# Decode attention on one core: wq loaded first through the key and value places, all heads' queries computed at once, and a new order for the last head

## The chip, the cores and the metric

One core of one Trainium2 chip. The metric is device time in microseconds (us) of one execution; runs of one kernel agree within about 0.2%. A run's span is from its first to its last instruction.

TensorE is PE, its weight loads PEld, VectorE DVE, ScalarE ACT, GpSimd POOL; SP only issues transfers.

## The reference, cut to what matters

One token goes through a pre-norm attention block with a cache, then a pre-norm ReLU block.

```python
B, Sq, D = 1, 1, 640
H, Sk, Dh = 32, 32768, 192            # k_cache, v_cache: [1, 32, 32768, 192] bf16, 403 MB each
x = A_x
q = (layernorm(x) @ wq).reshape(B, Sq, H, Dh).transpose(0, 2, 1, 3)      # wq [640, 6144]
scores = einsum("bhqd,bhkd->bhqk", q, k_cache) * Dh ** -0.5
o = einsum("bhqk,bhkd->bhqd", softmax(scores), v_cache)
h = x + o.transpose(0, 2, 1, 3).reshape(B, Sq, H * Dh) @ wo              # wo [6144, 640]
return h + relu(layernorm(h) @ w1) @ w2                                  # w1 [640, 1536], w2 [1536, 640]
```

## The kernel before

Each head's keys come in two loads of 6.29 MB (places `kt[0]`, `kt[1]`, 48 KB a partition), its values in four of 3.15 MB (`vt[0]`, `vt[1]` in turn). PE transposes part of the keys and computes their scores; DVE computes the other scores by multiply and sum. Eight chunks of scores a head go through ACT's exponential, then PE sums values weighted by them ("PV" below). One program per engine; `g.wait(label)` waits for the labelled step. wq is loaded in four parts of eight heads each, in rows of 3 KB, and each head's query row is computed during the head before it (QG = 8).

The transfers (all on SP's queue):

```python
# ... (cut: load(), rows())
        def keys(h, ld):
            if h > 0:
                g.wait("PV", h - 1, 4 * ld + 1)
                g.wait("scs", h - 1, 4 * ld + 3)
            load(kt[ld][:], rows(k_hd, h, P * JK * ld, JK), f"dk{ld}", "k", h, ld)

        def vals(h, ld):

            if ld == 1 and h > 0:
                g.wait("PV", h, 0)
            elif ld > 1:
                g.wait("PV", h, 2 * ld - 3)
            elif h > 0:
                g.wait("PV", h - 1, 5)
            if h < LAST:
                src = rows(v_hd, h, P * JK * (ld // 2), JK)[:, (ld % 2) * JL * Dh:(ld % 2 + 1) * JL * Dh]
            else:
                src = rows(v_hd, h, P * JL * ld, JL)
            load(vt[ld % NV][:], src, f"dv{ld % NV}", "v", h, ld)

        load(wq_v, wq_view[:, :, 0:QG * Dh], "dwq", "wq", 0)
        for h in range(LAST):
            keys(h, 0)
            if h > 0:
                vals(h - 1, NL - 1)
            vals(h, 0)
            if h % QG == QG - 1:
                gq = (h + 1) // QG
                g.wait("PV", h - 1, 3)
                load(wq_v, wq_view[:, :, gq * QG * Dh:(gq + 1) * QG * Dh], "dwq", "wq", gq)
            keys(h, 1)
            vals(h, 1)
            vals(h, 2)
            if h % 2 == 0:
# ... (cut) the last head, whose keys and values come in smaller pieces:
        for ld in range(NL - 1):
            if ld != 1:
                g.wait("PV", LAST - 1, 2 * ld + 1)
                g.wait("scs", LAST - 1, 2 * ld + 3)
            end_keys(ld, P * JL * ld, JL, ("dk0", "dke0", "dk1")[ld])
            if ld == 0:
                vals(LAST - 1, NL - 1)
            else:
                vals(LAST, ld - 1)
        k0 = P * JL * (NL - 1)
        at = []
        for i, jl in enumerate(ENDJ):
            at.append((k0, jl))
            end_keys(NL - 1 + i, k0, jl, f"dke{1 + i}")
            k0 += P * jl
        vals(LAST, NL - 2)
        i = 0
        for ld, (k0, jl) in enumerate(at):
            for c, (l, off, jc, *_) in enumerate(ends):
                if l == NL - 1 + ld:
                    g.wait("PV", LAST, 1)
                    load(v_tile(LAST, l)[:, off * Dh:(off + jc) * Dh],
                         rows(v_hd, LAST, k0, jl)[:, off * Dh:(off + jc) * Dh], f"dve{i}", "vc", LAST, c)
                    i += 1
        g.wait("PV", LAST, 3)
        load(w1_s, B_w1.rearrange("(c p) n -> p c n", p=P), "dw1", "w1")
        g.wait("PV", LAST - 1, 4)
        for i, (c0, c1) in enumerate(zip(W2_CUTS[:-1], W2_CUTS[1:])):
            load(w2_s[:, c0:c1], B_w2.rearrange("(c p) n -> p c n", p=P)[:, c0:c1], f"dw2_{i}", "w2", i)
        g.wait("y_row")
```

The query of a head, as a row, spread over all partitions and as columns:

```python
    def q_rows(g, h, turn=None):

        g.wait("at", "wq", h)
        hh = h % QG if turn is None else turn % QG
        pe_group(g, [mmul(mm[0:1, 0:Dh], ln_t["ln1"]["xn"][:, c:c + 1], wq_v[:, c, bass.ds(hh * Dh, Dh)],
                          start=(c == 0), stop=(c == DT - 1)) for c in range(DT)], ("q", h), "pe_act")

    def q_spread(g, h):
        g.wait("row", h)
        calls = [mmul(mm[:, 0:Dh], ones_row[:], row_e[0:1, Dh:2 * Dh], start=True, stop=True)]

        i = Dh
        for b in range(3):
            for e in range(2):
                for off in (Dh + b * (2 * P - Dh), b * (2 * P - Dh)):
                    calls.append(mmul(mm[:, i:i + 1], row_e[0:1, off + e:off + 2 * P:2], ones_row[0:1, 0:1],
                                      start=True, stop=True))
                    i += 1
        pe_group(g, calls, ("qs", h), "pe_act")
```

PE's program for the last head:

```python
    def pe_end(g):
        h = LAST
        transposes(g, h, 0)
        den_mm(g, h - 1)
        scores_pe(g, h, 0)
        for c in range(1, NC - 2):
            transposes(g, h, c)
            values(g, *((h - 1, NC - 3 + c) if c < 3 else (h, c - 3)))
            scores_pe(g, h, c)
            if c == 3:
                o_turn(g, h - 1)
        transposes(g, h, 6)
        values(g, h, 3)
        for c in (7, 8, 9):
            transposes(g, h, c)
            if c > 7:
                values(g, h, c - 4)
            scores_pe(g, h, c - 1)
        values(g, h, 6)
        scores_pe(g, h, 9)
        values(g, h, 7)
        den_mm(g, h)
        values(g, h, 8)
        values(g, h, 9)
        o_turn(g, h)
        project(g, h + 1)
        # ... (cut: the projection, the second norm, h1, y)
```

The softmax here doesn't subtract the row's maximum and nothing guards it: scores larger than these inputs give would overflow.

Of the kernel before, what the change touches and what calls it, by code (L numbers as in the profile page):

```python
# [7 lines left out]
A = mybir.AluOpType  # L8
# [72 lines left out]
def kernel(  # L81
# [20 lines left out]
    eps = 1e-5  # L102
# [8 lines left out]
    QG = 8  # L111
# [3 lines left out]
    NV = 2  # L115
    LAST = H - 1
    assert Sk % (P * JK) == 0 and NK == 2 and NL == 4 and 2 * Dh == 3 * P and H % QG == 0 and H % 2 == 0 and H >= 4

# [25 lines left out]
    wq_view = A_wq.rearrange("(c p) n -> p c n", p=P)  # L144
# [14 lines left out]
    wq_s = sbuf("wq_s", [P, DT * QG * Dh], bf16, 512)  # L159
# [6 lines left out]
    pA = [sbuf(f"pA{i}", [P, J], bf16) for i in range(4)]  # L166
    pB = [sbuf(f"pB{i}", [P, J], bf16) for i in range(4)]
    x_row = sbuf("x_row", [DT, P], bf16)
    ident_b = sbuf("ident_b", [P, P], bf16)
    ident_f = sbuf("ident_f", [P, P], f32)  # L170
    ones_row = sbuf("ones_row", [1, P], bf16)
# [4 lines left out]
    row_e = sbuf("row_e", [1, 3 * Dh], bf16)  # L176
# [22 lines left out]
    wq_v = wq_s[:].rearrange("p (c n) -> p c n", c=DT)  # L199
# [5 lines left out]
    w2_s = wq_s[:, 0:FT * D].rearrange("p (f n) -> p f n", n=D)  # L205
    assert DT * Dff <= JL * Dh and FT * D <= DT * QG * Dh
# [10 lines left out]
    names += [f"dk{i}" for i in range(NK)] + [f"dv{i}" for i in range(NV)] + ["dwq", "dwo", "dx", "dout"]  # L217
    names += [f"dke{i}" for i in range(4)] + [f"dve{i}" for i in range(4)] + ["dw1"] + [f"dw2_{i}" for i in range(3)]
# [6 lines left out]
    def dma_program(g):  # L225
# [6 lines left out]
        def keys(h, ld):  # L232
            if h > 0:
                g.wait("PV", h - 1, 4 * ld + 1)
                g.wait("scs", h - 1, 4 * ld + 3)
            load(kt[ld][:], rows(k_hd, h, P * JK * ld, JK), f"dk{ld}", "k", h, ld)

        def vals(h, ld):

            if ld == 1 and h > 0:  # L240
                g.wait("PV", h, 0)
            elif ld > 1:
                g.wait("PV", h, 2 * ld - 3)
# [5 lines that stand above are left out]
                src = rows(v_hd, h, P * JL * ld, JL)  # L249
            load(vt[ld % NV][:], src, f"dv{ld % NV}", "v", h, ld)  # L250

        load(wq_v, wq_view[:, :, 0:QG * Dh], "dwq", "wq", 0)
        for h in range(LAST):
            keys(h, 0)
            if h > 0:
                vals(h - 1, NL - 1)
            vals(h, 0)
            if h % QG == QG - 1:
                gq = (h + 1) // QG
                g.wait("PV", h - 1, 3)  # L260
                load(wq_v, wq_view[:, :, gq * QG * Dh:(gq + 1) * QG * Dh], "dwq", "wq", gq)
            keys(h, 1)
            vals(h, 1)
            vals(h, 2)
            if h % 2 == 0:
                if h > 0:
                    g.wait("prj", h)
                load(wo_s[:], wo_view[h // 2], "dwo", "wo", h // 2)
# [20 lines left out]
        vals(LAST, NL - 2)  # L289
# [10 lines left out]
        g.wait("PV", LAST - 1, 4)  # L300
# [8 lines left out]
    def pool_program(g):  # L309
        e = nc.gpsimd  # L310
        g.do(lambda: e.memset(ident_b[:], 0.0), "pool_act", ("ident0",))
        g.wait("ident0")
        g.do(lambda: e.affine_select(out=ident_b[:], in_=ident_b[:], compare_op=A.not_equal, fill=1.0, base=0,
                                     pattern=[[-1, P]], channel_multiplier=1), "pool_row", ("ident",))
        g.wait("x")
        g.do(lambda: e.sem_inc(sems["pool_pe"], 1) if not g.planning else None)
        book_relay(g, "x")
        relay(g, "wq", 0)
        def key(h, ld):
            relay(g, "k", h, ld)  # L320
            g.do(lambda: nc.gpsimd.sem_inc(sems["pool_dve"], 1))  # L321
            book_relay(g, "k", h, ld, sem="pool_dve")

        for h in range(LAST):
            key(h, 0)
            if h > 0:
                relay(g, "v", h - 1, NL - 1)
            relay(g, "v", h, 0)
            relay(g, "wq", h + 1)
            key(h, 1)  # L330
            relay(g, "v", h, 1)
            relay(g, "v", h, 2)
            relay(g, "W", h)
        for ld in range(NL - 1):
            key(LAST, ld)
            if ld == 0:
                relay(g, "v", LAST - 1, NL - 1)
            else:
                relay(g, "v", LAST, ld - 1)
        relay(g, "v", LAST, NL - 2)  # L340

    def relay(g, *label):
        if label[0] == "wq":
            if label[1] % QG == 0:
                g.wait("wq", label[1] // QG)
        elif label[0] != "W":
            g.wait(*label)
        elif label[1] % 2 == 0:
            g.wait("wo", label[1] // 2)
        g.do(lambda: nc.gpsimd.sem_inc(sems["pool_pe"], 1))  # L350
        book_relay(g, *label)
# [69 lines left out]
    def values(g, h, c):  # L421
# [3 lines left out]
        if h == LAST and ld >= NL - 1:  # L425
            g.wait("vc", h, c)
        elif off == 0:
            g.wait("at", "v", h, ld)
        g.wait("ep", h, c)
# [5 lines left out]
        a, b = pA[c % 4], pB[c % 4]  # L435
# [37 lines left out]
    def q_rows(g, h, turn=None):  # L473

        g.wait("at", "wq", h)
        hh = h % QG if turn is None else turn % QG
        pe_group(g, [mmul(mm[0:1, 0:Dh], ln_t["ln1"]["xn"][:, c:c + 1], wq_v[:, c, bass.ds(hh * Dh, Dh)],
                          start=(c == 0), stop=(c == DT - 1)) for c in range(DT)], ("q", h), "pe_act")

    def q_spread(g, h):  # L480
        g.wait("row", h)
        calls = [mmul(mm[:, 0:Dh], ones_row[:], row_e[0:1, Dh:2 * Dh], start=True, stop=True)]

        i = Dh
        for b in range(3):
            for e in range(2):
                for off in (Dh + b * (2 * P - Dh), b * (2 * P - Dh)):
                    calls.append(mmul(mm[:, i:i + 1], row_e[0:1, off + e:off + 2 * P:2], ones_row[0:1, 0:1],
                                      start=True, stop=True))
                    i += 1  # L490
        pe_group(g, calls, ("qs", h), "pe_act")
# [4 lines left out]
    def pe_head(g, h, turn=None):  # L496
        for c in range(NC):
# [13 lines left out]
            if c == 5:  # L511
                q_rows(g, h + 1, turn)
            if c == 6:
                q_spread(g, h + 1)
# [5 lines left out]
    def pe_start(g):  # L520
        g.wait("at", "x")
        g.wait("identf")
        pe_group(g, [lambda: pe.transpose(out=mm[:, 0:4].bitcast(bf16)[:, 0:DT], in_=x_row[:],
                                          identity=ident_b[0:DT, 0:DT])], ("xT",), "pe_dve")
        pe_norm(g)
        pe_group(g, [mmul(attT[:, 0:DT], ident_b[:], zero5[:], start=True, stop=False, skip_group_check=True)],
                 ("att0",))
        g.wait("xn", "ln1")
        g.wait("at", "wq", 0)
        q_rows(g, 0)  # L530
        q_spread(g, 0)

    def pe_end(g):
        h = LAST
        transposes(g, h, 0)
        den_mm(g, h - 1)
        scores_pe(g, h, 0)
        for c in range(1, NC - 2):
            transposes(g, h, c)
            values(g, *((h - 1, NC - 3 + c) if c < 3 else (h, c - 3)))  # L540
            scores_pe(g, h, c)
            if c == 3:
                o_turn(g, h - 1)
        transposes(g, h, 6)
        values(g, h, 3)
        for c in (7, 8, 9):
            transposes(g, h, c)
            if c > 7:
                values(g, h, c - 4)
            scores_pe(g, h, c - 1)  # L550
        values(g, h, 6)
        scores_pe(g, h, 9)
        values(g, h, 7)
# [36 lines left out]
    def exp_pe(g, h, c):  # L590
        jp = chunks(h)[c][3]
        g.wait("S", h, c)
        g.do(lambda: act.activation(out=pB[c % 4][:, 0:jp], in_=sp[:, 0:jp], func=F.Exp, scale=SCALE,  # L593
                                    accum_out=dsums[:, 2 * c + 1:2 * c + 2]), "act_pe", ("ep", h, c))

    def exp_dve(g, h, c):
# [5 lines left out]
        g.do(lambda: act.activation(out=pA[c % 4][:, 0:jd], in_=sc[c % NC][:, 0:jd], func=F.Exp, scale=SCALE,  # L602
                                    accum_out=dsums[:, 2 * c:2 * c + 1]), "act_pe", ("ed", h, c))

    def q_row(g, h):
        g.wait("q", h)
        g.do(lambda: act.copy(out=row_e[0:1, Dh:2 * Dh], in_=mm[0:1, 0:Dh]), "act_pe", ("row", h))  # L607
# [14 lines left out]
    def act_start(g):  # L622
        g.do(lambda: act.dma_start(out=x_row[:], in_=A_x.rearrange("b s (c p) -> (b s c) p", p=P)), "dx", ("x",), by=16)
        act_norm(g, "ln1")
        q_row(g, 0)

    def act_head(g, h):
        q_wide(g, h)
        for c in range(NC if h < LAST else NC - 2):
# [3 lines left out]
            if c == 5 and h < LAST:  # L633
                q_row(g, h + 1)
# [81 lines left out]
    def dve_start(g):  # L716
        for t, v in ((ones_row, 1.0), (mean_mat, 1.0 / D), (eps_t, eps), (row_e, 0.0), (ones_mat, 1.0), (dsums, 0.0),
# [3 lines left out]
        g.do(lambda: dve.tensor_copy(out=ident_f[:], in_=ident_b[:]), "dve_pe", ("identf",))  # L721
        g.wait("xT")
        g.chain(lambda: dve.tensor_copy(out=x_col[:], in_=mm[:, 0:4].bitcast(bf16)[:, 0:DT]), "dve_row")
        dve_norm(g, "ln1", x_col)
# [154 lines left out]
```

## Time and profile before

| | before |
|---|---|
| time, median (range) of 3 runs | 1923.72 us (1923.21 to 1923.9) |
| span of the profiled execution | 1923.6 us (its time: 1925.44) |
| busy: PE, DVE, ACT | 81%, 81%, 50% |
| the queue of SP: share of the 16 DMA engines' span | 99.6% |
| bytes read | 824.97 MB, 429 GB/s over the span |

The prediction below shows the lines on the middle and the end. Of the start, this is the timeline of PE and SP (start us, length us, engine, line, operation, out<-in, form, count, and in brackets the idle time before and what ended it):

```profile
8.69 0.96 PE L368 MATMUL mm<-wq_s,xn_ln 128*1 128x192 bf16 x5 [3.67 <-POOLq L350]
...
23.07 3.46 PE L387 MATMUL tp<-ident_f,kt 128*128 128x128 f32 x15 [12.39 <-POOLq L350]
...
27.82 0.90 PE L368 MATMUL sp<-qm,kT 128*128 128x2 bf16 x30 [1.29 <-ACT kT L587]
```

The first query comes out of the first part of wq at 8.7 us; PE then waits 12.4 us for head 0's keys ("POOLq" in a bracket is GpSimd's sequencer, which passes on to the others that a load has landed). The 30 score matmuls, each with a weight load of its own ("128*128": 128 rows by 128 columns), take 0.90 us, 30 ns each.

### The profile page before, as it was taken

The numbers are of one execution on the slowest core, as the hardware profiler recorded it, in microseconds if no ns is written. First come the engines' busy times: TensorE is split into PE (matmuls) and PEld (weight loads), VectorE is DVE, ScalarE is ACT, GpSimd is POOL, SyncE is SP. The second block draws the span as 40 slices with busy tenths as digits, with TensorE's granted clock in tenths as the row PEclk, the third lists the DMA queues.
The fourth block names the chain that finished last, engine by engine and source line by source line (L and its number), as shares of the span: only waits on it lengthen the run. The fifth ranks groups of instructions, "written<-read, shape, count | busy, mean of one in ns | idle before, by whom it ended". The sixth has DMA issues, their size and how long they took to land.

```text
span 1923.6 us, 36300 instructions
## 1 busy us (share of the span) xinstructions
PE 1554.4 (81%) x15899; PEld 1088.3 (57%) x15899; DVE 1560.5 (81%) x734; ACT 966.9 (50%) x2031; POOL 0.7 (0%) x6
## 2 busy tenths in 40 slices
PE   4878878777888788787777878878878788787897
PEld 3555555555555565555555655655656556555564
DVE  5878888878888798787787878978879788888885
ACT  3544545544555454454454545544545445544553
POOL 0000000000000000000000000000000000000000
PEclk8989898887888887888888888888788798898888
DMA  9999999999999999999999999999999999999997
GB/s 408 433 428 434 435 430 440 429 430 435 429 435 437 426 436 432 432 437 429 438 430 429 438 429 433 439 428 433 431 433 435 430 433 436 431 437 432 430 410 328
DMA packets 35864, 825.25 MB, mean 429 GB/s; under 512 B 3588, under 2 KB 5124, under 8 KB 11140
## 3 DMA queue, kind: packets, MB, share of 16 engines
q1 hardware_dynamic: 35834, 824.98, 99.6%
q8 instruction: 12, 0.20, 0.0%
q14 instruction: 8, 0.07, 0.0%
q10 hardware_dynamic: 10, 0.00, 0.0%
HBM read 824.97 MB, written 0.00 MB: 429 GB/s over the span
## 4 chain that ended last, share of the span: by engine, by line
DMA 55%; PE 35%; ACT 6%; DVE 3%; SPq 1%; issue 0%; POOLq 0%; DVEq 0%
DMA kt<-in_A_k_cache_dram 54%; PE o_ps L368 19%; PE tp L387 10%; ACT kT L587 6%; PE sp L368 4%; PE mm L368 2%; DVE pr L672 1%; DVE sc L675 1%; DMA vt<-in_A_v_cache_dram 1%; PE attT L368 1%; SPq L227 1%; ACT pA L602 0%; POOLq L350 0%; DVE o_pair L686 0%; ACT row_e L607 0%
## 5 line engine op out<-in xcount | busy, mean ns | idle before, releaser
L672 DVE TENSOR_TENSOR pr<-kt,qb 128x2304 f32<-128x2304 bf16 (+2 forms) x257 | 755.9, 2941 | 303.9 <-POOLq L321 278.7
L587 ACT COPY kT<-tp 128x1024 bf16<-128x1024 bf16 (+1 forms) x899 | 817.3, 989 | 321.3 <-PE tp L387 320.4
L387 PE MATMUL tp<-ident_f,kt 128*128 128x128 f32 x3459 | 578.1, 334 | 240.8 <-POOLq L350 238.6
L675 DVE TENSOR_REDUCE sc<-pr 128x12 f32<-128x2304 f32 (+2 forms) x257 | 755.3, 2939 | 8.9
L387 PEld LDWEIGHTS tp<-ident_f,kt 128*128 128x128 f32 x3459 | 501.8, 174 | 252.4 <-POOLq L350 244.0
L368 PE MATMUL o_ps<-vt,pB 128*2 128x384 bf16 x2286 | 459.2, 351 | 7.9 <-POOLq L350 7.1
L593 ACT ACTIVATE pB<-sp 128x20 bf16<-128x20 f32 (+2 forms) x258 | 47.8, 185 | 571.5 <-PE sp L368 571.5
L368 PE MATMUL o_ps<-vt,pA 128*2 128x384 bf16 x1778 | 330.6, 326 | 0.0
L368 PEld LDWEIGHTS o_ps<-vt,pB 128*2 128x2 bf16 x2286 | 187.6, 88 | 233.5 <-issue 92.2
L368 PE MATMUL sp<-qm,kT 128*128 128x2 bf16 x6918 | 214.5, 164 | 106.6 <-ACT kT L587 106.3
L368 PEld LDWEIGHTS sp<-qm,kT 128*128 128x128 bf16 x6918 | 192.5, 98 | 187.6 <-ACT kT L587 144.8
L368 PEld LDWEIGHTS o_ps<-vt,pA 128*2 128x2 bf16 x1778 | 150.0, 84 | 142.0 <-issue 3.5
L602 ACT ACTIVATE pA<-sc 128x12 bf16<-128x12 f32 (+2 forms) x257 | 53.4, 208 | 41.4 <-DVEq L65 40.5
L593 ACT ACTIVATION_READ_ACCUMULATOR pB<-sp 128x1 f32 x258 | 50.2, 194 | 0.0
L602 ACT ACTIVATION_READ_ACCUMULATOR pA<-sc 128x1 f32 x257 | 48.7, 190 | 0.0
L686 DVE TENSOR_SCALAR o_pair<-o_ps,rec 2x384 bf16<-2x384 f32 x32 | 19.4, 605 | 6.3 <-PE o_ps L368 1.7
L368 PE MATMUL mm<-wq_s,xn_ln 128*1 (+1 forms) x160 | 18.7, 248 | 3.7 <-POOLq L350 3.7
L680 DVE TENSOR_REDUCE rec<-mm 128x1 f32<-128x20 f32 x32 | 5.7, 179 | 16.3 <-PE mm L368 11.8
L368 PE MATMUL attT<-oT,wo_s 128*128 128x1 bf16 x465 | 16.4, 164 | 0.3 <-DVE oT L696 0.3
L368 PEld LDWEIGHTS mm<-dsums,ones_mat 128*128 128x128 f32 x64 | 15.1, 291 | 0.3 <-issue 0.3
L368 PEld LDWEIGHTS attT<-oT,wo_s 128*128 128x128 bf16 x465 | 14.5, 101 | 0.4 <-DVE oT L696 0.4
L368 PE MATMUL mm<-ones_row,row_e 1*128 1x1 bf16 x384 | 14.0, 159 | 0.0
(71 smaller groups left out, 145.4 us busy)
## 6 DMA issues: line engine op xcount, KB each, us to landing
vt<-in_A_v_cache_dram SPq DMA_DIRECT2D x127, 3072.0 KB, 18.8
kt<-in_A_k_cache_dram SPq DMA_DIRECT2D x62, 6144.0 KB, 32.4
kt<-in_A_k_cache_dram SPq DMA_DIRECT2D x3, 3072.0 KB, 18.3
wq_s<-in_A_wq_dram SPq DMA_DIRECT2D x4, 1920.0 KB, 22.5
wo_s<-in_A_wo_dram SPq DMA_DIRECT2D x16, 480.0 KB, 9.5
kt<-in_A_k_cache_dram SPq DMA_DIRECT2D x1, 1920.0 KB, 15.4
kt<-in_A_v_cache_dram SPq DMA_DIRECT2D x2, 960.0 KB, 22.4
kt<-in_B_w_dram SPq DMA_DIRECT2D x1, 1920.0 KB, 16.7
```

Source lines behind the costliest of these rows:

```text
L227: g.do(lambda: nc.sync.dma_start(out=dst, in_=src), sem, label, by=16)
L368: return lambda: pe.matmul(o, lhsT=w, rhs=r, **kw)
L387: calls.append(lambda b=b, o=o: pe.transpose(out=dst[:, b, :], in_=src[:, o:o + 2 * P].bitcast(f32), identity=ident_f[:]))
L587: g.do(lambda: act.copy(out=kT[c % 2][:, b0:b0 + nb, :], in_=src[:, 0:nb, :].bitcast(bf16)), "act_pe", ("cp", h, c, k))
L593: g.do(lambda: act.activation(out=pB[c % 4][:, 0:jp], in_=sp[:, 0:jp], func=F.Exp, scale=SCALE, accum_out=dsums[:, 2 * c + 1:2 * c + 2]), ...
L602: g.do(lambda: act.activation(out=pA[c % 4][:, 0:jd], in_=sc[c % NC][:, 0:jd], func=F.Exp, scale=SCALE, accum_out=dsums[:, 2 * c:2 * c + 1 ...
L672: g.chain(lambda: dve.tensor_tensor(out=pr[:, 0:j1 - j0, :], in0=src[:, (off + j0) * Dh:(off + j1) * Dh].rearrange("p (j d) -> p j d", d=D ...
L675: g.chain(lambda: dve.reduce_sum(out=sc[c % NC][:, j0:j1], in_=pr[:, 0:j1 - j0, :], axis=X), "dve")
L680: g.chain(lambda: dve.reduce_sum(out=rec[:, 0:1], in_=mm[:, 0:2 * NCM], axis=X), "dve")
L686: g.do(lambda: dve.tensor_scalar_mul(out=o_pair[:, :, 1, :], in0=o_ps[0:2, 0:2 * Dh].rearrange("q (i d) -> q i d", i=2), scalar1=rec[0:2, ...
```

## The change

Its intent: load all of wq at the start in long rows, using places that are still free, so that no small rows come later and no query work lies in the heads; let the last head's second value load go as soon as its place is free; halve the third, and reorder the last head so that PE does not wait for it. The core of the diff:

```diff
-    wq_view = A_wq.rearrange("(c p) n -> p c n", p=P)
+    wq_view = A_wq.rearrange("(p c) n -> p (c n)", p=P)
-    pA = [sbuf(f"pA{i}", [P, J], bf16) for i in range(4)]          # pB likewise
+    pA = [sbuf(f"pA{i}", [P, J], bf16) for i in range(NB)]         # NB = 5
+    x_pc = sbuf("x_pc", [P, DT], bf16)
+    qe = sbuf("qe", [HE, 2 * H], bf16)                             # HE = Dh // 2 = 96
+    wq_c = [kt[1][:, c * H * Dh:(c + 1) * H * Dh] for c in range(DT - 1)] + [vt[1][:, 0:H * Dh]]
-    w2_s = wq_s[:, 0:FT * D].rearrange("p (f n) -> p f n", n=D)
+    w2_s = sbuf("w2_s", [P, FT, D], bf16, 512)
@@ transfers
         def keys(h, ld):
+            elif ld == 1:
+                g.wait("att0")
         def vals(h, ld):
-            if ld == 1 and h > 0:
+            if ld == 1 and h == LAST:
+                g.wait("vfree")
+            elif ld == 1 and h > 0:
                 g.wait("PV", h, 0)
-        load(wq_v, wq_view[:, :, 0:QG * Dh], "dwq", "wq", 0)
+        n = (DT - 1) * H * Dh
+        load(kt[1][:], wq_view[:, 0:n], "dwq0", "wq", 0)
+        load(vt[1][:, 0:H * Dh], wq_view[:, n:n + H * Dh], "dwq1", "wq", 1)
-            if h % QG == QG - 1:
-                gq = (h + 1) // QG
-                g.wait("PV", h - 1, 3)
-                load(wq_v, wq_view[:, :, gq * QG * Dh:(gq + 1) * QG * Dh], "dwq", "wq", gq)
-        vals(LAST, NL - 2)
+        g.wait("PV", LAST, 1)
+        src = rows(v_hd, LAST, P * JL * (NL - 2), JL)
+        n = J * Dh
+        load(vt[0][:, 0:n], src[:, 0:n], "dv0", "v", LAST, NL - 2)
+        load(vt[0][:, n:2 * n], src[:, n:2 * n], "dvh", "vh")
@@ PE
+    def queries(g):
+        for c in range(DT):
+            if c == 0 or c == DT - 1:
+                g.wait("wq", min(c, 1))
+            calls = [mmul(o_ps[0:HE, 2 * h + e:2 * h + e + 1], wq_c[c][:, h * Dh + e:(h + 1) * Dh:2],
+                          ln_t["ln1"]["xn"][:, c:c + 1], ...)
+                     for h in range(H) for e in range(2)]
@@ pe_start: ... queries(g), then att0; q_rows and its ACT copy are gone, q_spread reads qe
@@ pe_end
+        transposes(g, h, 1)
         scores_pe(g, h, 0)
+        values(g, h - 1, NC - 2)
+        values(g, h - 1, NC - 1)
+        pe_group(g, [mmul(attT[0:1, 500:501], ident_b[0:1, 0:1], zero5[0:1, 0:1], start=False, stop=True,
+                          skip_group_check=True)], ("vfree",))
+        scores_pe(g, h, 1)
+        ... (cut) transposes and scores run ahead, so that before values(4) only scores 8 and 9 are open:
+        transposes(g, h, 9)
+        values(g, h, 4)
+        scores_pe(g, h, 8)
+        scores_pe(g, h, 9)
+        for c in (5, 6, 7):
+            values(g, h, c)
@@ ACT
         g.do(lambda: act.dma_start(out=x_row[:], in_=A_x.rearrange("b s (c p) -> (b s c) p", p=P)), "dx", ("x",), by=16)
+        g.do(lambda: act.dma_start(out=x_pc[:], in_=A_x.rearrange("b s (p c) -> (b s p) c", p=P)), "dx2", ("x_pc",), by=16)
```

## The prediction

> **What bounds the kernel now.** I read the page first, for the busy shares. The transfers are the full resource: TensorE (PE) and VectorE (DVE) are busy 81% of the span, the one DMA queue 99.6%.
>
> ```profile
> q1 hardware_dynamic: 35834, 824.98, 99.6%
> HBM read 824.97 MB, written 0.00 MB: 429 GB/s over the span
> ```
>
> The key and value caches are 2 x 32 heads x 32768 x 192 x 2 bytes = 805.3 MB of these 825; wq and wo are 7.9 MB each, w1 and w2 2.0 MB each. A busy queue can still be one that waits for buffers, so next I read the chain of work that ended last, in order of time (start, length, what). The loads of the second half of a head's keys recur in it; start plus length is when one landed.
>
> ```profile
> 306.64 33.81 DMA kt<-in_A_k_cache_dram
> ...
> 365.21 33.38 DMA kt<-in_A_k_cache_dram
> ...
> 423.82 38.73 DMA kt<-in_A_k_cache_dram
> ...
> 489.70 30.90 DMA kt<-in_A_k_cache_dram
> ...
> 547.73 32.12 DMA kt<-in_A_k_cache_dram
> ```
>
> They landed at 340.45, 398.59, 462.55, 520.60 and 579.85, so 58.14, 63.96, 58.05 and 59.25 us apart. A head moves 25.17 MB, and every other head 0.49 MB of wo too: 25.17 MB in 58.1 us is 433 GB/s, and 25.66 MB in 59.25 us is 433 GB/s again. The same two intervals recur to the last head. A loop held by waits would not price half a megabyte of wo at exactly its bytes; so the middle is bound by bytes, and no work of an engine there is worth anything. The third load came after one of the four wq loads (1.97 MB in rows of 3 KB): 63.96 - 59.25 = 4.7 us, or 417 GB/s. At 433 it would have been 4.54 us. **The small rows of wq cost about 0.17 us a load, 0.7 us in all.**
>
> What remains outside the middle is the start and the end. Windows of the end (last two columns: DMA share, GB/s):
>
> ```profile
> 1868.00:1878.00 10.00, 9.29 (x80) 5.37 (x78) 9.56 (x7) 5.90 (x11) 0.00 (x0) 0.88 0.86 336
> 1902.00:1913.00 11.00, 10.83 (x100) 5.81 (x98) 0.48 (x3) 3.96 (x13) 0.00 (x0) 1.00 1.03 399
> 1913.00:1924.00 11.00, 5.18 (x146) 4.47 (x146) 2.24 (x13) 0.56 (x2) 0.00 (x0) 0.74 0.04 14
> ```
>
> In the first, (433 - 336) x 10 us = 0.97 MB is missing: 2.2 us without transfers. Windows of 1 us place it at 1870 to 1874 (221 and 25 GB/s at its bottom). The issues on the queue say why:
>
> ```profile
> 1848.12 0.43 SPq L227 DMA_DIRECT2D kt<-in_A_k_cache_dram  x1
> 1872.17 0.33 SPq L227 DMA_DIRECT2D vt<-in_A_v_cache_dram  x1
> 1872.54 1.72 SPq L227 DMA_DIRECT2D kt<-in_A_k_cache_dram  x3
> 1878.36 0.33 SPq L227 DMA_DIRECT2D vt<-in_A_v_cache_dram  x1
> ```
>
> For 24 us nothing is issued: the last head's second value load waits for that head's first values matmuls, although the matmuls that free its buffer are the previous head's last. Transfers then run without a gap to about 1913.3. The chain's last part:
>
> ```profile
> 1878.36 19.60 DMA vt<-in_A_v_cache_dram
> ...
> 1898.05 4.26 PE o_ps L368 x16
> ...
> 1912.86 0.62 DVE o_pair L686
> ...
> 1915.59 1.67 PE o_ps L368 x60
> ...
> 1917.61 1.73 PE attT L368 x60
> ```
>
> The third value load of the last head lands at 1897.95; PE idles 2.5 us before it, then has 14.8 us of work until its last values matmul (1912.84), then 10.8 us of short steps to the end. The last piece of w2 lands at about 1915.0 (issued 1904.7, 10.3 us to landing), 2.6 us before the matmuls on w2 begin. So the end is PE's, with the transfers close behind.
>
> **What the Trainium skill says.**
> - DMA: Bandwidth & Descriptors, section Where 436 GB/s comes from: sixteen ports give 435.2 GB/s. The trace's 433 agrees; the section's remark that HBM binds near 358 does not hold in this trace, with one core running.
> - Same page, section Why small descriptors are slow: a fixed overhead per packet. Agrees in kind: 3-KB rows at 417 against 433 GB/s; it is small at this size.
> - TensorE: Matmul & The Clock Gate, section What's actually happening: an idle window of about 3.4 us halves the clock. The trace has a granted clock of 0.50 from 1898 to 1901, just after the 2.5-us idle, and the 16 values matmuls took 4.26 us there against 2.7 at full clock; the exact threshold no view shows.
>
> **The change, part by part.**
>
> *All of wq first* (6.29 MB in 48-KB rows into the key place, 1.57 MB in 12-KB rows into a value place). No byte is saved: 5.90 MB, or 13.6 us at 433, move from the middle to the start, and head 0's keys land at about 36.4 instead of 22.97. Every later load moves early by what left the middle. Gain: the 0.7 us above. Added: x once more as 128 rows of 10 bytes, 8 per DMA engine, which I guess at 0.1 to 0.5 us. Net about -0.4.
>
> *The queries at once*: 320 matmuls with 96-column weights and one moving column. The like matmuls of the scores (sp, 30 in 0.90 us in the timeline) run at 30 ns each, so 9.6 us. The first 256 can start at about 18 (2.2 to the first byte, 14.5 for the bytes, 1.3 to landing); the last 64 wait for the second load at about 22, behind the first 256 which end near 25.7; done near 28. The second key load waits for this, but the queue still holds head 0's first keys and values until about 42. So nothing stalls.
>
> *Per head*, PE loses the five matmuls on wq and most of the 13 of the spreading (0.57 + 0.25 + 0.44 us in the timeline of head 0), ScalarE (ACT) a copy of 0.3 us. All beside transfers: 0 us on the end.
>
> *vfree*: the one-element matmul after the previous head's last values, near 1859 in the old timeline (after the scores at 1853.7, two values groups of 2.7 us). The load then goes out 13 us earlier, with two loads still ahead of it: the hole is closed, -2.2 us for all later transfers.
>
> *Halved third value load, new order, five probability buffers*: the old order waits at 1898.05 for the whole load. With the shift of -2.6 (0.4 + 2.2) the whole lands at 1895.3, its first half (1.57 MB, 3.6 us) at 1891.7. PE no longer waits for it: the last head's fourth key piece lands at about 1885.2 (1888.0 before), then, by old durations, transposes 2.1, values(3) 3.1, transposes 1.2; the copies of ACT (2.2 us) hold the scores to about 1893.8; scores 0.6, transposes 0.9: values(4) start near 1895.3. Left from there: 16 + 16 + 10 + 10 + 8 + 4 values matmuls at 163 ns = 10.4 us, scores(8) and (9) 0.8, the wait for the exponential between them 0.4, the sum 0.3: 12 us, so the last values end near 1907.4 instead of 1912.84. The last value pieces land by about 1903, in time. DVE's last scores move from 1899.0 to about 1897.5: in time. The 10.8 us of short steps stay: 1918.2. w1 lands near 1907.4, needed near 1910.2; w2 ends near 1912.4, its matmuls would end near 1913.9. The end is still PE's, with 1.5 us in hand.
>
> *w2 in a buffer of its own*: removes a wait already fulfilled; 0.
>
> **Sum**: the profiled span goes from 1923.6 to 1918.2, -5.4 us: about 2.6 from the transfers, 2.8 from the shorter PE tail after them. The times lie 0.1 above the span: 1918.3.
>
> **Rivals.**
> 1. *The transfers become the end's bound.* w2 with 1280-byte rows lands last. For: the 399 GB/s of the second window, and only 1.5 us in hand. It sets a floor: 1912.4 + 0.4 for the last matmuls + 4.3 to the end = 1917.1. No faster PE tail gets below it unless the transfers themselves gain more.
> 2. *The clock.* If PE idles before values(4) and drops to half clock as at 1898, 1.6 us or more of the gain is lost: 1920. For: the old trace does this often. Against: the new order fills the idle.
> 3. *Head 0.* Between 22.97 and the landing of head 1's first keys (76.2) 22.5 MB moved, 52.0 us at 433: 1.2 us were lost, I think since head 0's third value load (issued at 48.8) came just too late behind work at half clock. The whole stretch now comes 13.4 us later with the same order, and another phase of the clock: from -1.2 to +1.5.
> 4. *Queries stall the second key load*: only if a query matmul takes over 75 ns ((42 - 18) us / 320). At 160 ns it would add some 27 us (1945), still within 2%. The scores' 30 ns speak against it.
> 5. *Everything hidden*: only wq's rows count, and the tail is eaten by DVE or ACT: 1921 to 1923. The hole in the transfers speaks against it.
>
> **Range and chances.** 1918.3 with the clock (+1.6), head 0 (-1.2 to +1.5) and the floor of the transfers gives 1915.7 to 1921.2. Two per cent is 38 us; nothing but rival 4 at an extreme comes near: same 0.98.
>
> **What would show it.** Right: intervals of 58.1 and 59.25 us in the middle without one of 64; first key landing near 36; no window below 400 GB/s between 1865 and 1878; the second value load of the last head issued near 1859; last values near 1907 to 1908; w2's matmuls not waiting for w2. Wrong: a hole in the transfers before 60 us; PE waiting on a load between values(4) and values(9); half clock there; head intervals other than these.

## The result, and the profile after

| | before | after |
|---|---|---|
| time, median (range) | 1923.73 us (1923.21 to 1923.9), 4 runs | 1930.01 us (1929.44 to 1931.05), 4 runs |
| ratio, 95% interval | | 1.0034 [1.0016, 1.0051] |
| span of the profiled execution | 1923.6 | 1927.6 |

The change made the kernel 6.3 us slower; 1918.3 was predicted, and the range ended at 1921.2. Ratios here are the mean time of one kernel's runs over that of the other's of the same rounds, so not quite the ratio of the medians quoted. A later call repeated it: 1930.20 us (5 runs), ratio 1.0030 [1.0016, 1.0044].

**The middle is as predicted.** The chain of the changed kernel, the same recurring load (start, length):

```profile
447.89 33.51 DMA kt<-in_A_k_cache_dram
506.51 32.98 DMA kt<-in_A_k_cache_dram
564.60 34.15 DMA kt<-in_A_k_cache_dram
```

Landings at 481.40, 539.49 and 598.75: 58.09 and 59.26 us apart, and no interval of 64 anywhere. So whatever was lost was lost at the start or the end.

**The start is where it went.** The timeline of the changed kernel (columns as before):

```profile
1.54 0.36 ACTq L643 DMA_DIRECT2D x_pc<-in_A_x_dram  x1
...
18.91 0.16 DVE L721 TENSOR_REDUCE st_ln<-x_pc 128x1 f32<-128x5 bf16 x1 [16.13 <-DMA x_pc<-in_A_x_dram]
...
21.51 20.64 PE L369 MATMUL o_ps<-xn_ln,kt 128*96 128x1 bf16 x256
...
42.01 5.26 PE L369 MATMUL o_ps<-xn_ln,vt 128*96 128x1 bf16 x64
...
47.34 0.33 SPq L230 DMA_DIRECT2D kt<-in_A_k_cache_dram  x1
...
48.07 3.24 PE L388 MATMUL tp<-ident_f,kt 128*128 128x128 f32 x15
```

Three things are to be seen. The second of the two x loads (x_pc, which the norm reads), issued at 1.54, lets DVE start only at 18.9. The query matmuls have the form 128*96, and 256 of them take 20.64 us: 81 ns each, not 30. And the second key load goes out at 47.34, when they are done. Windows of the two kernels (us, busy time and count of PE, PEld, DVE, ACT, POOL, then PE clock, DMA share, GB/s); first before, then after:

```profile
43.00:49.00 6.00, 6.00 (x44) 2.91 (x42) 5.72 (x3) 0.83 (x1) 0.00 (x0) 0.89 0.91 393
70.00:75.00 5.00, 4.58 (x48) 2.51 (x46) 1.81 (x1) 0.99 (x6) 0.00 (x0) 1.00 0.92 398
```

```profile
43.00:49.00 6.00, 5.73 (x68) 5.64 (x68) 0.33 (x1) 0.60 (x3) 0.00 (x0) 1.00 0.43 131
70.00:75.00 5.00, 5.00 (x55) 3.19 (x53) 4.75 (x2) 0.77 (x5) 0.00 (x0) 1.00 0.42 123
```

Two holes, that is stretches without transfers: the queue runs empty near 43 us and again near 71. In windows of 2 us, 2.3 MB are missing between 42 and 50 (5.3 us at 433 GB/s) and 1.9 MB between 70 and 76 (4.4 us). The second hole follows from the first delay: head 0's work starts at 48.07, when the queries end, though its keys were there long before; the third value load of head 0 waits for 25 us of that work and goes out at 73.5, while the queue is empty from 71 on. Head 1's second key load lands at 129.44 instead of 105.50, 23.9 us later, of which wq's moved bytes are 13.6: **10.3 us lost at the start**. (Some 0.9 of it comes back in the middle, where wq's small rows are gone: 0.7 was predicted.)

**The end came out faster, as predicted, and another wait ends it.** Chain of the end, then PE's last matmuls on w2, after:

```profile
1912.36 10.47 DMA w_s<-in_B_w_dram
...
1922.88 0.44 PE attT L369 x10
```

```profile
1920.48 0.94 PE L369 MATMUL attT<-h1T,w_s 128*128 128x1 bf16 x30 [0.48 <-DMA w_s<-in_B_w_dram]
1922.05 1.25 PE L369 MATMUL attT<-h1T,w_s 128*128 128x1 bf16 x30 [0.63 <-DMA w_s<-in_B_w_dram]
```

From the landing of the last but one head's second key load (1820.88 before, 1830.31 after) to the end of the span it is 102.7 us before and 97.3 after: 5.4 us gained. But PE now waits for w2 (the "DMA w_s" in the brackets; w_s is the profile's short name for w2's buffer), which it did not before. In the two traces: +9.4 from the start and middle, -5.4 at the end, +4.0 in all; the other 2.3 of the 6.3 us are that the profiled execution of before is a slow one (1.7) and the changed kernel's a fast one (0.6).

### The profile page after: what moved, and what is told of

Its sections match the earlier page's. It is cut to its first block, busy times and chain, and to the rows that moved or that the text cites. A ratio compares the mean times of both kernels' runs of the same rounds, so it can differ in the third digit from the quotient of the medians.

```text
span 1927.6 us, 36148 instructions
## 1 busy us (share of the span) xinstructions
PE 1562.3 (81%) x15900; PEld 1102.7 (57%) x15900; DVE 1560.0 (81%) x732; ACT 956.8 (50%) x2000; POOL 1.0 (0%) x6
## 4 chain that ended last, share of the span: by engine, by line
DMA 55%; PE 32%; DVE 7%; ACT 5%; SPq 1%; issue 1%; POOLq 0%; DVEq 0%; ACTq 0%
DMA kt<-in_A_k_cache_dram 53%; PE o_ps L369 18%; PE tp L388 9%; ACT kT L610 5%; PE sp L369 3%; DVE pr L691 3%; DVE sc L694 3%; SPq L230 1%; DMA x_pc<-in_A_x_dram 1%; DMA w_s<-in_B_w_dram 1%; PE attT L369 1%; PE mm L369 0%; POOLq L351 0%; DVEq L65 0%; ACTq L642 0%
## 5 line engine op out<-in xcount | busy, mean ns | idle before, releaser
L388 PE MATMUL tp<-ident_f,kt 128*128 128x128 f32 x3459 | 584.2, 337 | 234.2 <-POOLq L351 232.7
L388 PEld LDWEIGHTS tp<-ident_f,kt 128*128 128x128 f32 x3459 | 508.4, 175 | 241.1 <-POOLq L351 238.0
L369 PE MATMUL o_ps<-xn_ln,kt 128*96 128x1 bf16 (+1 forms) x316 | 22.4, 208 | 0.0
L369 PEld LDWEIGHTS o_ps<-xn_ln,kt 128*96 128x96 bf16 (+1 forms) x316 | 22.2, 176 | 0.1
L715 DVE TENSOR_SCALAR oT<-mm,odd 128x3 bf16<-128x3 f32 x32 | 7.1, 223 | 10.5 <-PE mm L369 8.1
## 6 DMA issues: line engine op xcount, KB each, us to landing
kt<-in_A_v_cache_dram SPq DMA_DIRECT2D x2, 960.0 KB, 18.3
```

Source lines behind the costliest of these rows:

```text
L369: return lambda: pe.matmul(o, lhsT=w, rhs=r, **kw)
L388: calls.append(lambda b=b, o=o: pe.transpose(out=dst[:, b, :], in_=src[:, o:o + 2 * P].bitcast(f32), identity=ident_f[:]))
L715: g.do(lambda: dve.tensor_scalar_mul(out=oT[:], in0=mm[:, 0:3], scalar1=odd[:]), "dve_pe", ("oTc", h))
```

## The experiments

My theory (W): the queries' weight loads of 96 columns take 80 ns instead of 30, keep the second key place for 26 us, and so make both holes. Rivals: x's late landing (X); the step of two elements or the large place makes the loads slow (S); wq first is itself the loss, since head 0 starts later (O); for the end, that it only looks shorter because the transfers come late.

All times, each with the kernel before in the same rounds (medians 1924.89, 1924.47 and 1924.42):

| run | median us (range) | ratio to before [95%] |
|---|---|---|
| a_xfirst | 1927.38 (1927.26 to 1929.28) | 1.0016 [1.0002, 1.0029] |
| b_w128 | 1921.26 (1920.20 to 1922.40) | 0.9980 [0.9967, 0.9994] |
| c_both | 1921.18 (1920.62 to 1921.84) | 0.9981 [0.9968, 0.9995] |
| e_tail | 1919.81 (1919.45 to 1920.24) | 0.9974 [0.9960, 0.9987] |
| f_wq | 1933.82 (1932.96 to 1936.03) | 1.0049 [1.0036, 1.0063] |
| d_vfree | 1923.89 (1922.00 to 1924.55) | 0.9996 [0.9982, 1.0009] |
| k_wo0 | 1919.64 (1919.27 to 1919.77) | 0.9974 [0.9960, 0.9988] |
| p_probe | 1931.85, one run, state unknown | |
| after_again | 1930.20 (1929.95 to 1930.56) | 1.0030 [1.0016, 1.0044] |
| h_wo0 | 1920.56 (1919.95 to 1921.20) | 0.9980 [0.9966, 0.9993] |
| g_whole | 1922.38 (1921.84 to 1922.62) | 0.9989 [0.9975, 1.0002] |
| n_novfree | 1922.53 (1920.09 to 1923.18) | 0.9989 [0.9975, 1.0002] |

Five runs each but for the probe, all correct.

**a_xfirst**: x first, on the queue of wq.

```diff
@@ ACT: both x loads taken out; SP, ahead of wq:
+        load(x_pc[:], A_x.rearrange("b s (p c) -> (b s p) c", p=P), "dx2", "x_pc")
+        load(x_row[:], A_x.rearrange("b s (c p) -> (b s c) p", p=P), "dx", "x")
```

> The changed kernel with one edit: x is loaded on the same queue as wq and ahead of it, so that its 128 ten-byte rows no longer wait beside 48-KB rows. Theory W (the 96-column weight loads of the queries, 80 ns each, hold the key place): x lands near 4 us instead of 18.9, the queries start when wq's first load lands (near 19), still take 80 ns each, and end near 45 instead of 47.1; the hole in the transfers stays, only some 2 us shorter; time about 1928.2 (1930.0 before the edit). Rival X (the late x is the cause): the queries fit in, the hole near 44 us goes, time 1921 or less. Rival O (wq first is itself the loss, since head 0 starts later): 1929 to 1930.

Measured: 1927.38, ratio 1.0016 against the changed kernel's 1.0030, so some 2.7 us faster than it. The queries now wait for wq, not for x, and are as slow as before:

```profile
19.19 20.64 PE L371 MATMUL o_ps<-xn_ln,kt 128*96 128x1 bf16 x256 [13.77 <-DMA kt<-in_A_wq_dram]
```

They end at 44.9 instead of 47.2, and the hole remains, shorter: 273 GB/s from 42 to 50 us. The late x is a part, not the cause.

**b_w128**: 128 weight columns instead of 96.

```diff
-            calls = [mmul(o_ps[0:HE, 2 * h + e:2 * h + e + 1], wq_c[c][:, h * Dh + e:(h + 1) * Dh:2],
+            def wide_w(h, e):
+                t, o = (kt[1], c * H * Dh + h * Dh + e) if c < DT - 1 else (vt[1], h * Dh + e)
+                n = P if h < H - 1 else HE
+                return n, t[:, o:o + 2 * n - 1:2]
+            calls = [mmul(o_ps[0:wide_w(h, e)[0], 2 * h + e:2 * h + e + 1], wide_w(h, e)[1],
```

> The changed kernel with one edit: the query matmuls load 128 weight columns instead of 96, in the same steps of two elements (the 32 extra columns belong to the next head and their results are not used; only the last head keeps 96). Theory W: one such matmul takes about 30 ns, as those of the scores do, so the first 256 end near 29.5 and the rest near 31.5, before the key place is needed near 42; both holes (43 to 49, 71 to 75 us) go or shrink below 2 us in sum; time about 1920.5. Rival S (the step of two elements, or reading the large key place, makes the loads slow, not the number of columns): still about 80 ns or more each, time about 1930 or worse. Rival X (late x): they still start at 21.5, and 2 us of that are x's; time above 1927. Rival O: 1929 to 1930.

Measured: 1921.26, 9 to 10 us faster than the changed kernel, and for the first time faster than before. More columns, loaded in less time:

```profile
21.70 6.32 PE L369 MATMUL o_ps<-xn_ln,kt 128*128 128x1 bf16 x219
...
31.91 1.95 PE L369 MATMUL o_ps<-xn_ln,vt 128*128 128x1 bf16 x64
...
33.92 0.33 SPq L230 DMA_DIRECT2D kt<-in_A_k_cache_dram  x1
```

219 in 6.32 us: 29 ns each. The ten matmuls that keep 96 columns in this run, the last head's, still show the long form (218 ns from start to end of one, against 165 with 128 columns; these durations overlap, so they are longer than the pace). The second key load goes out at 33.9 instead of 47.3. Of the holes, from 43 to 49 nothing is left, and a remainder stands between 62 and 67:

```profile
43.00:49.00 6.00, 4.77 (x70) 4.37 (x68) 5.82 (x3) 4.56 (x10) 0.00 (x0) 1.00 1.05 455
62.00:67.00 5.00, 4.78 (x54) 3.27 (x52) 4.72 (x3) 1.85 (x6) 0.00 (x0) 1.00 0.83 310
```

The step of two elements, the place, the order of the loads and the time at which x lands are all unchanged, so S, X and O fall together as the cause of the loss: it was the number of columns, 96 instead of 128; widths between them were not tried. (Between 28.0 and 30.8 us PE waited for nothing that the profile puts it down to; a gap of 2.5 us stands at the same instruction in c_both. In both runs one 16-KB packet of the queue that the profile calls "instruction" moves as the gap begins, between 28.25 and 28.5 us here and between 25.5 and 26 there, where the gap begins at 25.6. So a wait for instructions is likely; no run tested it. The gap costs nothing there.)

**c_both**: both edits together, with nothing else changed.

> Both edits: x first and 128 columns. Theory W: the queries end near 28 to 30, long before they are needed, so nothing beyond the 128 columns alone: 1920.5, within 0.7 of that run. Rival X: clearly faster than 128 columns alone, by 2 us or more. Rival O: 1929 to 1930.

Measured: 1921.18, as b_w128. With 128 columns x's lateness is hidden, as W has it.

**p_probe**: how late small rows come beside wq. x is read once more, unused, as a probe; the result stays correct.

```diff
# ... (cut: the tiles and the semaphore)
+        g.do(lambda: act.dma_start(out=x_16[:], in_=A_x.rearrange("b s (p c) -> (b s p) c", p=16)), "dx3", ("x_16",), by=16)
@@ GpSimd
+        g.wait("x")
+        g.do(lambda: e.memset(mark_row[:], 0.0))
+        g.wait("x_16")
+        g.do(lambda: e.memset(mark_16[:], 0.0))
```

> The changed kernel with a third, unused load of x, 16 rows of 80 bytes[...], issued between the two others on the same queue; GpSimd, idle then, waits for the 5-row load and for this one and writes a tile after each, so that both landings show. Theory R (each row takes its turn with one 48-KB row of wq on its engine): the 5-row and the 16-row load, one row per engine each, land within one or two rows of wq (1.8 us each), near 4 to 6 us, while the 128-row load, eight per engine, still lands near 19. Rival F (x on its own queue waits for the whole of wq's first load whatever its rows): all near 19. Time no concern: 1928 to 1932.

Measured: neither theory holds. The timeline shows the two marks and DVE's start:

```profile
2.34 0.10 POOL L328 MEMSET mark_row<- 128x1 f32 x1 [0.40 <-DMA x_row<-in_A_x_dram]
...
9.25 0.10 POOL L330 MEMSET mark<- 128x1 f32 x1 [6.81 <-DMA x<-in_A_x_dram]
...
20.23 0.16 DVE L729 TENSOR_REDUCE st_ln<-x_pc 128x1 f32<-128x5 bf16 x1 [17.46 <-DMA x_pc<-in_A_x_dram]
```

The 5-row load, issued first, had landed at 2.3, when wq's transfers had only begun (the windows show none of its bytes before 2 us). The 16-row load took 7.7 us from its issue, the 128-row load 18.3. If rows are dealt evenly to the 16 DMA engines, that is one row and eight rows on each, and a 48-KB row takes an engine about 1.8 us (an estimate: 433 GB/s over 16 engines), so the 7.7 us are about four rows of wq. Small rows do wait for large ones of another queue, and more rows wait longer, so "all near 19" is wrong; but one turn per row is too quick. The Trainium skill (DMA: Bandwidth & Descriptors, section Queues, rings and completion order) has each DMA engine go round the queues packet by packet; that fits the direction, while the first row's 7.7 us would need some rows queued ahead inside the engine, which no run here shows. The exact rule stays open.

**f_wq**: the changed kernel with the old end (its diff takes back the lines that e_tail, below, adds).

> The changed kernel with the end undone: wq first, large rows and queries at once as in the change, the last head's order, waits and whole loads as before. Theory (start and end add up): the start costs some 10 us (two holes in the transfers), the end gave back 5 of it; so 1930.0 + 4 to 5 = 1934.5, some 10 us above the kernel before. The hole of 2 us near the last head's second value load is back. Rival (transfers that come late let the engines catch up, so the old end costs less here): 1931 to 1932.

Measured: 1933.82, ratio 1.0049: the start costs 9.4 us with the old end, as the trace's 9.4. The end gives back 3.7 us there (1.0049 against 1.0030; 2.9 against the first call's 1.0034), less than the 4 to 5 expected, and one expectation failed: no hole at the last head. The issues of the second value load and the load before it:

```profile
1855.96 0.43 SPq L230 DMA_DIRECT2D kt<-in_A_k_cache_dram  x1
1879.12 0.33 SPq L230 DMA_DIRECT2D vt<-in_A_v_cache_dram  x1
```

It still waits 23 us for the last head's first values, but the load before it lands at 1883.48, 4.4 us after this issue, against 1.5 us in the kernel before (1872.17 and 1873.68), and the transfers run on at 423 GB/s from 1876 to 1890. The engines are further ahead of the transfers there. The heads without query work are the likely reason; that was not tested alone.

**d_vfree**: only the signal that frees the place, in the kernel before.

```diff
@@ vals: as in the change
+            if ld == 1 and h == LAST:
+                g.wait("vfree")
@@ pe_end, in the old loop after values
+            if c == 2:
+                pe_group(g, [mmul(attT[0:1, 500:501], ident_b[0:1, 0:1], zero5[0:1, 0:1], ...)], ("vfree",))
```

> The kernel before with only the one-element matmul after the previous head's last values, which lets the last head's second value load go; order, whole loads and four probability buffers as before. Theory: the load is issued near 1863 instead of 1872, the hole of 2.2 us is gone, and all later loads and the PE work behind them come 2.2 us earlier: 2 us faster than before, so some 2.5 us slower than the whole new end (1919.8). Rival (PE's end was late anyway, the transfers are hidden): within 0.7 of before.

Measured: 1923.89, ratio 0.9996 [0.9982, 1.0009]. In its trace the load is issued at 1864.58 and the hole is gone (427 GB/s from 1868 to 1878, 336 before), as expected; but over the runs it is worth 0.8 us, with an interval from -1.7 to 3.5. Inconclusive; the 2 us that I read off one trace of before are not shown to be there in its other runs.

**e_tail**: the whole new end on the kernel before (signal, halves, order, five buffers: the lines of the change's diff under `vals`, after `vals(LAST, NL - 2)`, under `pe_end` and for `NB`; wq, x and queries as before, w2 still in wq's place).

> The kernel before with only the end of the change (freed place told by the one-element matmul, halved third value load, new order of the last head, five probability buffers); wq as before. Theory: the end of the changed kernel is worth what its trace shows, y ends 40.4 us after the landing of the last head's third key load instead of 45.7: 5.2 us, so about 1918.5. The transfers have no hole of 2 us near 1872, and w2 is what the last matmuls wait for. Rival (the end only looks shorter in the changed kernel because its transfers come late and the engines have caught up): gain under 2.5 us, 1921.2 or more.

Measured: 1919.81, 5 us faster than before. The rival falls. Its chain ends on w2, like that of the changed kernel:

```profile
1902.47 10.38 DMA wq_s<-in_B_w_dram
...
1912.89 0.44 PE attT L376 x10
```

**g_whole**: e_tail with the third value load whole.

```diff
-        load(vt[0][:, 0:n], src[:, 0:n], "dv0", "v", LAST, NL - 2)
-        load(vt[0][:, n:2 * n], src[:, n:2 * n], "dvh", "vh")
+        load(vt[0][:, 0:2 * n], src[:, 0:2 * n], "dv0", "v", LAST, NL - 2)
```

> The kernel before with the new end (1919.8), but the last head's third value load whole again. Theory: its landing, near 1896, holds values(4), which start at 1894.2 with the halves; the last values then end 1.9 us later and the matmuls on w2 start 1.9 us later, past the landing of w2, which they wait for now: +1.5, so 1921.3. Rival (w2's landing sets the end anyway): +0 to 0.4.

Measured: 1922.38, 2.9 us slower than e_tail by the ratios. The chain goes through the whole load again:

```profile
1880.90 14.88 DMA vt<-in_A_v_cache_dram
...
1895.87 4.44 PE o_ps L375 x16
```

The direction is as expected, the size larger: the sixteen matmuls after the wait took 4.44 us, as in the kernel before (4.26), instead of 2.7 in e_tail (1894.18 to 1896.87). So the halves are worth more than the wait alone. With the wait PE also loses its clock in these traces: the granted clock is 0.50 from 1897 to 1899 us in g_whole, after a wait of 1.3 us for the load, and 1.00 from 1894 to 1903 in e_tail.

**n_novfree**: e_tail with the second value load waiting for the last head's first values again.

```diff
-            if ld == 1 and h == LAST:
-                g.wait("vfree")
-            elif ld == 1 and h > 0:
+            if ld == 1 and h > 0:
```

> The kernel before with the new end (1919.8), but the second value load waits for the last head's first values again, as before the change. Theory: in the new order those values end near 1871, when the loads ahead have about 1 us left; with 1.5 to 2 us to the first bytes the hole is 0.5 to 1.5 us, and the end is set by transfers, so +1: 1920.8. Rival (no hole any more, the signal is worth nothing in the new order): 1919.8.

Measured: 1922.53, but in two groups: spans of 1918.2 and 1918.4, and 1920.7, 1921.2 and 1921.3; e_tail's five lie from 1917.7 to 1918.4. The profiled run is of the quick group (1918.2; the load was issued at 1870.65, and 383 GB/s from 1868 to 1876 against e_tail's 432 show a hole of about 0.9 us). So in the new order the signal is worth 0 to 3 us from run to run. What sets the group is not shown: the slow ones have no trace.

**k_wo0** and **h_wo0**: head 0's wo load ahead of its third value load, in e_tail and in c_both.

```diff
             vals(h, 1)
+            if h == 0:
+                load(wo_s[:], wo_view[0], "dwo", "wo", 0)
             vals(h, 2)
-            if h % 2 == 0:
-                if h > 0:
-                    g.wait("prj", h)
+            if h % 2 == 0 and h > 0:
+                g.wait("prj", h)
```

> The best so far (the kernel before with the new end, 1919.8) with the first wo load moved ahead of head 0's third value load, which waits for head 0's first values. If the transfers run dry there for some 1.2 us, as the bytes between the landings of head 0's and head 1's keys say, the 0.49 MB (1.1 us) of wo fill it: 1918.8. Rival (no dry stretch there; the 1.2 us are a slow stretch of transfers): 1919.8, no change.

> Both edits of the queries (x first, 128 columns) and the first wo load ahead of head 0's third value load. With wq first the rest of the change now costs nothing, but that run lay 1.4 us above the new end alone. Theory: a dry stretch of about 1 us is left near 66 us, where the third value load of head 0 waits for its first values; wo fills it: 1920.2. Rival (the 1.4 us come from the start itself, loads of 48-KB rows that ramp up later): 1921.2, no change.

Measured: 1919.64 (e_tail 1919.81) and 1920.56 (c_both 1921.18), both within noise. In k_wo0, head 1's second key load lands 82.5 us after head 0's first (105.74 and 23.24); in e_tail, which is the same but for wo, 83.1 (106.38 and 23.32); in the kernel before 82.5 (105.50 and 22.97). One trace differs from another by as much as the edit gains, 0.6 us at most: the 1.1 us that wo was to fill are not there. So the 1.2 us missing at head 0 in the kernel before are not shown to be a dry stretch that a small load can fill.

**after_again**: the changed kernel once more.

> The changed kernel as it is, beside the others of this call and once more against the kernel before: 1929.5 to 1931, some 5 to 6.5 us above the kernel before. A second trace should have the same two holes in the transfers (43 to 49 and 71 to 75 us) if they come from the queries and not from chance; if chance, they lie elsewhere or are gone.

Measured: 1930.20, and its trace has both holes in the same places: 139 GB/s from 43 to 49 and 64 from 70 to 75.

The versions that beat both kernels, with intervals below 1: e_tail and k_wo0 (1919.8 and 1919.6), then h_wo0, c_both and b_w128 (1920.6 to 1921.3). g_whole, n_novfree and d_vfree are not clear of the kernel before. That the repaired start (c_both) does not beat the old start (e_tail) although wq's small rows are gone is open: 1.4 us by the medians, some 0.5 of it in the key landings of the two traces (1821.91 against 1821.37), the rest in the end, and all near the spread of the runs.

## Why the prediction was wrong, point by point

- **The step that failed: "The like matmuls of the scores ... run at 30 ns each, so 9.6 us".** The score matmuls have 128 weight columns, the queries 96, and these took 81 ns each: 320 of them 25.9 us. I compared the two by what they compute and not by the form of their weights. The Trainium skill had it (TensorE: Matmul & The Clock Gate, section Weight-path perf modes): the fast weight load is on only with 128 weights and a type other than FP32; without it, section LDWEIGHTS (loading the stationary operand) gives columns / 1.2 in ns, an estimate of 80 for 96. The trace (81) and b_w128 (29 for 128) agree with both.
- **"So nothing stalls" fell with it.** The second key load waited until 47.3 for its place, 5 us after the queue was empty. Rival 4 had named this, with its threshold (75 ns); I gave it no weight in the range. Its own sum counted only the one wait: at 81 ns it gives 2 us (18 + 25.9 - 42). The rest of the loss is that the queries began at 21.5 and not at 18 (3.5 us, the greater part since x was late: they began at 19.2 in a_xfirst), and the second hole (4.4 us). The columns were enough, though: b_w128 leaves x late and undoes the loss. The second hole (head 0 starting at 48 instead of 36.4, so its third value load late) was not foreseen.
- **"Added: x once more ... 0.1 to 0.5 us"**: its bytes are nothing, but it landed at 18.9 beside wq's long rows. I priced its time on the engines and not its wait; a_xfirst puts it at some 2.7 us in the time of the kernel while the queries are slow, c_both at nothing when they are fast.
- **Middle**: right: 58.1 and 59.26, no 64.
- **"Per head ... 0 us on the end"**: right on the transfers. But f_wq has no hole at the last head even with the old wait, so the -2.2 of the signal is not the changed kernel's to gain, and d_vfree and n_novfree leave it between nothing and some 3 us.
- **End, -2.2 and -2.8**: the sum was right (5.0 by e_tail, 5.4 in the traces), the parts are not shown: the halves alone are 2.9, the signal on the old order 0.8 with an interval from -1.7 to 3.5. That the sum agrees so well is in part luck. Rival 1 came true: w2's landing ends the chain in every version with the whole new end, and in n_novfree; only g_whole's chain ends on PE.
- **"The times lie 0.1 above the span"**: wrong; some 1.84. I compared a median of other runs with the span of a slower execution. That is 1.7 us of the miss. (The range's upper end is also 0.2 below its own terms, 1918.3 + 1.6 + 1.5 = 1921.4, and its lower end lies below the floor of 1917.1 that rival 1 sets, unless the transfers gain too.)
- The miss of 11.7 us adds up: start and middle +9.4 in the traces instead of -0.4 (9.8), the end -5.4 instead of -5.0 (-0.4), span and time 1.7, and the profiled execution 0.6 quicker than the median.

## What to carry to other kernels

Take the duration of a new matmul from one of the same weight form, columns first: here 96 columns cost nearly three times as much as 128, and loading 32 useless columns saved 9 us. When a borrowed buffer holds something, the work that empties it is on the path of the next transfer: price it with its slowest plausible rate, and follow the first delay to the waits behind it. A small transfer issued beside long rows can land when they do; put it ahead on the same queue.

## What the Trainium skill lacked or had wrong

- TensorE: Matmul & The Clock Gate: what it says of weight loads was right (81 ns a matmul at 96 columns, 29 at 128), but the rule that follows for narrower weights, to read up to 128 columns and drop the rest, is not drawn there; here it took 9 to 10 us off the kernel.
- DMA: Bandwidth & Descriptors: its account of turns between queues gives no figure for a small load beside long rows: here 7.7 us from issue for 16 rows and 18.3 for 128, beside rows of 48 KB.
- DMA: Bandwidth & Descriptors, section Where 436 GB/s comes from: that HBM binds loads near 358 GB/s is said there without the condition that the pair's other core streams too, which stands only elsewhere on that page; with one core running, 429 GB/s were the mean over the whole span and 433 held in the middle.
- Runtime: NRT & Kernel Launch, section Instruction fetch mechanics: it has no figure for a fetch of instructions that an engine has to wait for. The gap of 2.5 to 2.8 us in the run of fast query matmuls (b_w128, c_both), which the profile puts down to no wait, begins as one 16-KB packet of the instruction queue moves; that the fetch is its cause is not shown.
